# First k projections by contraction block, dummy matmuls ahead of them, 128-row transposes of the bias rows, and a newly planned order

## The chip, the core and the metric

The kernel runs on one core of one Trainium2 chip. The metric is the device time of one execution in microseconds, as the median of three runs. A core has five engines that run their own instruction streams side by side: TensorE (PE, matmuls; its weight loads are shown apart as PEld), VectorE (DVE), ScalarE (ACT), GpSimd (POOL) and SyncE (SP), which here does nothing but issue DMA transfers. The streams meet only at semaphores, and each is executed in order.

## The reference, cut to what matters

The input x has 2048 rows of 448 features. Two branches are computed from it and mixed row by row with a gate.

```python
g = sigmoid((x * gate_w).sum(-1, keepdims=True))

# branch A: 16 heads of 28, four segments of 512 rows
q, k, v = x @ wq, x @ wk, x @ wv
for s in range(4):
    p = softmax(q_s k_s^T * scale + causal mask)
    a_dot = p @ v_s
    a_mem = (phi(q_s) @ M) / (phi(q_s) @ z + 1e-6)
    o_s = sigmoid(beta) * a_mem + (1 - sigmoid(beta)) * a_dot
    M, z = M + phi(k_s)^T v_s, z + phi(k_s).sum(rows)
a = o @ wo

# branch B: a two-layer network over the row axis
h = layernorm(x)
u = gelu(h^T @ w1 + b1)        # 448 x 1792
b = (u @ w2 + b2)^T            # 2048 x 448

out = g * a + (1 - g) * b
```

## The kernel before

**A planner makes the order.** The program is written as about 1300 operations, each with an engine (some with a choice of two), the resources that it reads and writes, a cost in ns, a priority, and for a DMA its number of bytes. `Sched.plan` is a list scheduler: it walks through time, gives each engine the ready operation of lowest priority number, counts a TensorE operation double before `COLD` (3200 ns from its start), adds `SWITCH` where TensorE changes between full and packed matmuls, and lets a DMA land by one channel of 290 bytes per ns (L240 to L243). `SHIFTS` adds a number to the priority of single operations by name. The outcome is a fixed order of each engine's instructions, with the semaphore waits that the dependencies need. Nothing is decided on the chip: an engine whose next instruction waits stands still, with all that is behind it.

**The work.** Names as they are used below, with n counting tiles or groups:

- `ldx`, `ldwk`, `ldwq`, `ldwv`, `ldgw`, `ldb1`, `ldb2`, `ldbeta`, `ldwo`: loads of x (tiles of 128 rows), the weights, the gate's weights, biases and the rest. A weight of 448 rows comes in contraction chunks of 128 rows, the last one overlapping (`C0`): `ldwk0` brings chunks 0 and 1, `ldwk1` chunk 2, `ldwkb` chunk 3. `load_w` (L485) issues them on SP, with `ldwkb` alone on ACT's queue.
- `dtx1_0` to `dtx3_1` (`transpose_x`, L495): x transposed by DMA, 512 rows to a chunk (a chunk's three contraction blocks in `_0`, the fourth in `_1`). The first 512 rows are transposed by TensorE instead: `trx0_0` (row tiles 0 and 1) and `trx0_1` (tiles 2 and 3), each into two PSUM banks that `xTcp0_..` copies to SBUF (`transposes_0`, L628; DVE for contraction blocks 0 and 1, ACT for 2 and 3).
- `warm`, `warm2` (L595): seven and two dummy matmuls of 512 columns over a constant, into a bank that is not read.
- `padk`, `padx`, `padq` (L609): DVE spreads the weights' heads of 28 columns over 32, in chunks (`padk0` chunks 0 and 1, `padk1` chunk 2, `padk2` chunk 3).
- `prk`, `prq`, `prx` (`proj_d`, L655): projections of k, of q, and of the last heads of both, four heads to a group, by four matmuls over the contraction chunks. For the first 512 rows k is done in two halves of 256 (`prk0_n` and `prk0_nh`). One operation holds a group's four matmuls, so none of them starts before all chunks of the weights and both copies of the half are there. `cpk`, `cpq` evict them.
- `prt` (`do_v`, L743): v and the gate's sum, `wvx` carrying the gate's weights as column 448. They come from `gstage`, four rows of 128, by a TensorE transpose `gtr` (`do_gw`, L766) and the copies `gw`, `gwb`. `btr` (`do_small`, L805) does the same for the 30 rows of biases in `bstage`.
- `gk`, `gq`: heads of 28 columns leave the last four columns of each 32 free; these hold the heads that group 3 lacks, which are gathered through DRAM (four stores, then loads `_h0` to `_h2`), in two batches from SP.
- `ek`, `mk`, `phk`, `tk` and `eq`, `mq`, `phq`: phi of k and q on ACT and DVE, k's transposed by DMA (`tk`). `mst`, `msta`, `mstc`: the memory.
- `sc`, `exp`, `mask`, `pv`, `mem`, and the DVE chain `ta` to `ot`: attention by pairs of units (a unit is four heads of a segment). A pair's scores are filled in five steps `sc_0` to `sc_4`, each over the same four banks 0 to 3, which `exp` on ACT must have read before the next step; `mask` on POOL clears what is above the diagonal.
- `bns`, `bna`, `vpe`, `rstd`, `nmr`, `ln`: the layer norm, in place on x, on DVE (`rstd` on POOL).
- `u` and `y` (`mm1`, `mm2`): branch B, u by 14 blocks of 16 matmuls (one for each tile of x after `ln`), y by 16 of 14, with `gsq`, `gvh`, `garg`, `gth`, `gelu` as its GELU. Their weights pass through three ring slots, 1 MB (`ldw1_0` to `_6`) or 0.9 MB (`ldw2_0` to `_7`) a load. `wo`, `ag`, `fin`, `out` finish a row tile.

**The order around the change.** On TensorE: `warm`, `trx0_0`, `warm2`, `trx0_1`, then the k projections of the first 512 rows, half 0 (three groups) and half 1 (two), `prx0_3`, `prq0_0`, `prq0_1`, `gtr`, the last k half and the first v tiles. On SP: x tile 0, `ldwk0`, `ldwk1`, x tiles 2 and 3, wq, wv, the gate's weights, `dtx1`, x tiles 4 to 15, the biases, `ldbeta`, one part of wo, `ldw1_0`, then `tk0_0`, `tk0_1`, `dtx2`, `ldw1_1`, `dtx3_0` and the gathers. Until then, banks are dealt out in turn, 0 to 3 (`next_bank`, L589).

## Time and profile before

| what | value |
|---|---|
| median of the runs | 180.11 us (180.07 to 180.22) |
| the profiled execution, first to last instruction | 180.4 us |
| DVE busy | 151.0 us, 84% |
| ACT busy | 131.3 us, 73% |
| SP's queue: share of the 16 DMA engines' time | 53.1% |

The profile is of one execution of its own. Times in it count from its first instruction. In a list by time a row has the start, the length, the engine, the line of the kernel, the operation, what is written from what, and how many instructions are merged; in brackets is the idle time of the engine before it and what ended that. A matmul's length has some time of the pipeline in it, so rows of neighbours overlap. An SPq or ACTq row is the issue of a transfer, not the transfer.

The loads that feed the ring, as the page has them (KB each, median us from issue to landing):

```profile
t<-in_B_w_dram SPq DMA_DIRECT2D x7, 1024.0 KB, 6.2
```

### The profile page before, as it was taken

To read this page: it belongs to the slowest core of one execution; us is meant where nothing else is said; L and a number is where in the kernel's file an instruction comes from. 1 tells how busy PE (TensorE), PEld (TensorE's weight loads), DVE (VectorE), ACT (ScalarE), POOL (GpSimd) and SP (SyncE) were. 2 spreads that over 40 slices of the span, in tenths; PEclk is the share of its full clock that TensorE was granted. 3 is DMA by queue.
4 is the path that set the end of the run, shared out by engine and by line. 5 is a ranking of instruction groups with operands and counts; after the bars stand their busy time and mean duration, and the time that the engine had idled before them with its cause. 6 is when DMAs were issued, how large, how long until landed. Compare 5 with 4: busy or idle time off the path is not lost.

```text
span 180.4 us, 3443 instructions
## 1 busy us (share of the span) xinstructions
PE 174.0 (96%) x1300; PEld 83.3 (46%) x1313; DVE 151.0 (84%) x335; ACT 131.3 (73%) x161; POOL 71.1 (39%) x93
## 2 busy tenths in 40 slices
PE   8799998999999999999999999999999999999993
PEld 3454443444544544344544444444445444545562
DVE  2579989999898899999999797999798998983131
ACT  2267798899958999998999998987496977104100
POOL 7023111835503252436562727655632458520000
PEclk9999999999999999999999999999999999999999
DMA  5999997595581757121715241128731008394001
GB/s 160 261 292 300 129 271 162 136 253 134 156 231 33 221 155 153 25 51 40 207 57 147 71 136 29 48 66 228 202 89 37 14 4 254 95 320 125 22 29 51
DMA packets 49552, 24.32 MB, mean 135 GB/s; under 512 B 14384, under 2 KB 49296, under 8 KB 49536
## 3 DMA queue, kind: packets, MB, share of 16 engines
q1 hardware_dynamic: 49312, 23.93, 53.1%
q8 instruction: 10, 0.16, 0.4%
q10 hardware_dynamic: 224, 0.17, 0.3%
q14 instruction: 6, 0.05, 0.1%
HBM read 18.59 MB, written 2.36 MB: 116 GB/s over the span
## 4 chain that ended last, share of the span: by engine, by line
PE 67%; DVE 14%; ACT 13%; DMA 2%; issue 1%; SPq 1%
PE t L1032 23%; PE t L1004 20%; ACT t L905 8%; PE t L659 5%; PE t L984 5%; PE t L896 5%; PE t L933 5%; DVE t L839 3%; DMA t<-in_A_x_dram 2%; ACT t L1008 2%; DVE t L855 1%; PE t L749 1%; DVE t L684 1%; ACT t L1019 1%; DVE t L716 1%
## 5 line engine op out<-in xcount | busy, mean ns | idle before, releaser
L905 ACT ACTIVATE t<-t 128x2048 bf16<-128x2048 f32 x40 | 75.3, 1884 | 8.8 <-PE t L896 8.7
L908 POOL TENSOR_SCALAR_AFFINE_SELECT t<-t 128x512 bf16<-128x512 bf16 x64 | 46.9, 734 | 61.2 <-ACT t L905 50.6
L1004 PE MATMUL t<-t 128*128 128x448 bf16 x224 | 46.3, 353 | 0.4 <-DVE t L727 0.3
L1032 PE MATMUL t<-t 128*128 128x448 bf16 (+1 forms) x238 | 46.3, 342 | 0.3 <-DVE t L959 0.2
L1032 PEld LDWEIGHTS t<-t 128*128 128x128 bf16 x238 | 22.3, 98 | 19.7 <-issue 2.5
L1004 PEld LDWEIGHTS t<-t 128*128 128x128 bf16 x224 | 20.5, 98 | 20.8 <-issue 3.1
L659 PE MATMUL t<-t 128*128 128x512 bf16 (+1 forms) x118 | 27.6, 373 | 0.3
L1037 DVE SCALAR_TENSOR_TENSOR t<-t 128x448 bf16<-128x448 f32 (+1 forms) x17 | 10.9, 646 | 12.6 <-PE t L1032 12.6
L964 POOL TENSOR_TENSOR t<-t 128x448 bf16<-128x448 f32 x12 | 15.5, 1295 | 10.5 <-DVE t L962 10.5
L659 PEld LDWEIGHTS t<-t 128*128 128x128 bf16 x124 | 12.3, 104 | 11.7 <-issue 0.6
L896 PE MATMUL t<-t 28*128 28x512 bf16 (+3 forms) x256 | 15.8, 301 | 0.3 <-ACT t L763 0.2
L990 ACT ACTIVATE t<-t 128x448 bf16<-128x448 f32 x11 | 7.8, 726 | 10.6 <-PE t L984 10.5
L749 PE MATMUL t<-t 128*128 128x449 bf16 x64 | 14.4, 354 | 0.3 <-DVE t L684 0.3
L984 PE MATMUL t<-t 128*128 128x448 bf16 x64 | 13.3, 353 | 0.0
L949 DVE STREAM_TRANSPOSE t<-t 128x512 f32<-128x512 f32 x16 | 11.3, 704 | 0.9 <-PE t L933 0.8
L970 DVE STREAM_TRANSPOSE t<-t 128x512 bf16<-128x512 bf16 x16 | 11.1, 694 | 0.7 <-POOL t L964 0.7
L933 PE MATMUL t<-t 128*32 128x512 bf16 (+3 forms) x256 | 11.6, 302 | 0.0
L896 PEld LDWEIGHTS t<-t 28*128 28x128 bf16 x256 | 4.4, 92 | 14.0 <-ACT t L905 9.1
L1019 ACT ACTIVATE t<-t 128x448 f32<-128x448 f32 x14 | 8.1, 590 | 2.0 <-DVE t L1016 1.9
L947 DVE STREAM_TRANSPOSE t<-t 128x512 f32<-128x512 f32 x12 | 8.3, 694 | 1.4 <-remote 1.0
L1008 ACT ACTIVATE t<-t 128x448 f32<-128x448 f32 x14 | 8.9, 642 | 0.8 <-PE t L1004 0.8
L848 POOL TENSOR_TENSOR t<-t 128x4 f32<-128x4 f32 x4 | 4.5, 1138 | 12.4 <-DVE t L846 12.4
(81 smaller groups left out, 211.7 us busy)
## 6 DMA issues: line engine op xcount, KB each, us to landing
t<-in_B_w_dram SPq DMA_DIRECT2D x7, 1024.0 KB, 6.2
t<-in_B_w_dram SPq DMA_DIRECT2D x8, 896.0 KB, 5.3
out_dram<-t SPq DMA_DIRECT2D x15, 112.0 KB, 2.7
t<-in_A_x_dram SPq DMA_DIRECT2D x3, 448.0 KB, 5.0
t<-in_A_wo_dram SPq DMA_DIRECT2D x4, 98.0 KB
t<-in_A_wq_dram SPq DMA_DIRECT2D x1, 336.0 KB, 4.9
t<-in_A_wv_dram SPq DMA_DIRECT2D x1, 336.0 KB, 4.9
spare_heads<-t SPq DMA_DIRECT2D x8, 32.0 KB
```

Source lines behind the costliest of these rows:

```text
L659: last = e.matmul(bank(b)[:, 0:n], wqk[:, c, 4 * G : 4 * G + 4, :].rearrange("p h j -> p (h j)"), xT[0:CK, c, tc * 512 + t0 : tc * 512 + t ...
L749: last = e.matmul(bank(b)[:, 0 : D + 1], xT[0:CK, c, t * 128 : t * 128 + 128], wvx[0:CK, c, 0 : D + 1], start=(c == 0), stop=(c == NCT - 1 ...
L896: last = e.matmul(bank(hl)[:, c0 : c0 + w], kT[r, hg, s * 512 + j * 128 : s * 512 + j * 128 + 128], qT[r, hg, s * 512 + 128 * j : s * 512 ...
L905: op("ACT", lambda e: e.activation(pslot(g), ps[:, 0:4, :], ACT.Exp, scale=SCALE), reads=R_bank[0:4], writes=[g.res], take=g, name=f"exp{p ...
L908: op("POOL", lambda e, c0=c0: e.affine_select(pslot(g)[:, :, c0 : c0 + 128], pslot(g)[:, :, c0 : c0 + 128], pattern=[[0, 4], [1, 128]], co ...
L933: last = e.matmul(bank(cb)[32 * hl : 32 * hl + 32, 128 * j : 512], vaug[:, 4 * s + j, 32 * h : 32 * h + 32], pslot(P_fill[u // 2][f])[:, h ...
L949: dv(lambda e: e.transpose(t2[:, 0, :], bank(cb)[:, 0:512]), [bres(cb)], [R_tt[tb][0]], "ta", 630, use=(cb,))
L964: op("POOL", lambda e: e.tensor_tensor(o3, n3[0], n3[1], op=ALU.add), reads=R_tt[tb], writes=[R_ob[tb]], name=f"o{u}", cost=1280, port=Tru ...
L984: last = e.matmul(bank(b)[:, 0:D], oT[:, hg, T * 128 : T * 128 + 128], wo_sb[:, hg, :], start=(hg == 0), stop=(hg == NHG - 1), skip_group_ ...
L1004: op("PE", lambda e, st=st: e.matmul(bank(b)[:, 0:D], w1c[:, st, f2 * 128 : f2 * 128 + 128], xh[:, st, :], start=(st == 0), stop=(st == NT ...
L1008: op("ACT", lambda e: e.activation(gg[:, q, :], bank(b)[:, 0:D], ACT.Square, bias=b1s[:, ft : ft + 1], scale=math.sqrt(GC)), **buse(b), re ...
L1032: op("PE", lambda e, ft=ft: e.matmul(bank(b)[:, 0 : c1 - c0], w2c[:, ft, t2_ * 128 : t2_ * 128 + 128], uT[:, ft, c0:c1], start=(ft == 0), ...
```

## The change

Seven things are edited:

1. `warm2` goes. `fill` issues `NFILL` = 6 dummies of 256 columns, each an operation of its own and of the highest priority number, released at 3000 ns of the plan.
2. `do_k_first` takes the place of the first three `do_k`: for each of the three groups an operation for contraction chunks 0 and 1, one for chunk 3 and one for chunk 2, each waiting for its own chunk of weights and its own copy of x alone.
3. `xTcp0_..` may run on either ACT or DVE. The banks of the first operations are dealt out by the list `EARLY`.
4. `bstage` and `gstage` have 128 rows, cleared by DVE, and `btr` and `gtr` are plain matmuls against columns of the identity, over 128 rows and into float32.
5. `ldwk1` is issued on ACT.
6. The planner's model of DMA and of the start: `COLD` 5500, the channel 350 bytes per ns with a stretch around 2400 ns in which 1200 ns are added, a least time for each DMA (`dmin`: 5900 for the w1 loads, 5300 for w2), other bytes and costs for the transposing DMAs.
7. A new `SHIFTS` of some 150 entries. With 6 it makes another order of nearly all operations.

The new order begins, on TensorE: `warm`, `trx0_0`, six fills, the three pieces of k group 0, `trx0_1`, the pieces of groups 1 and 2 interleaved, the three k groups of half 1, `prq0_0`, `prq0_1`, `prk1_0`, `prx1_3`, `prq0_2`, `prk1_1`, `prk1_2`, `prq1_1`, `prq1_2`, `prx0_3`, four matmuls of `u0`, `prq1_0`, `btr`, `gtr`, four of `u1`, `prk2_0`, `prk2_1`, seven v tiles, four of `u0`, `prt7`, `sc0_0`, twelve of `u2` and `u0`, `sc0_1`, four of `u2`, seven of `u1`, `sc0_2`, and after ten more the last matmul of `u0`.

On SP: `ldx0`, `ldwk0`, `ldx2`, `ldwq0`, `dtx1_1`, `ldwqb`, `ldwvb`, `ldwv0`, `dtx1_0`, `ldx8`, `ldgw`, `ldx4`, `ldb1`, `ldb2`, `ldw1_0`, `dtx2_0`, `dtx2_1`, `ldbeta`, `ldwo1`, `ldwo3`, `ldgwb`, `ldw1_1`, `ldx12`, `dtx3_1`, `tk0_0`, `gk0_3`, `gq0_1`, `gq0_2`, `gq0_3`, `gk0_2`, `ldwo2`, `tk0_1`, `ldwo0`, `gq0_0`, `gk0_1`, `ldw1_2`, `gk0_0`, `tk0_2`, `gq0_h0` to `_h2`. On ACT the Exp of q `eq1_3`, which reads what `gq0_h0` to `_h2` bring, stands between `exp0_1` and `exp0_2`. On POOL the four `rstd` come ahead of the first mask.

```diff
...
 SWITCH = 97.0
+NFILL = 6
 HOLD = 2500.0
-COLD = 3200.0
+COLD = 5500.0
+DMA = (350.0, 1000.0, 950.0, 2400.0, 1200.0)
 LAT = {"PE": 163.0, "ACT": 120.0, "DVE": 83.0, "POOL": 50.0, "SP": 0.0}
...
             if o.nbytes:
-                chan = max(chan, t + 1090.0) + o.nbytes / 290.0
-                o.end = max(t + 1900.0, chan + 850.0)
+                before = chan
+                chan = max(chan, t + DMA[1]) + o.nbytes / DMA[0]
+                if before <= DMA[3] < chan:
+                    chan += DMA[4]
+                o.end = max(t + o.dmin, chan + DMA[2])
             else:
...
 SHIFTS = (
-    ("cpk3_3", 15.1), ("dtx3_0", -0.43), ("dtx3_1", 146.0), ("gk2_1", 0.63), ("gq0_0", 7.37), ("gq3_h2", 215.59),
-    ("gth7", 7.61), ("gvh10", 14.61), ("gvh11", -0.19), ("ldbeta", 0.27), ("ldw1_3", 235.85), ("ldwk0", -64.28),
...
+    ("b2c", -26.38), ("b2g1", -67.36), ("bna15", 153.62), ("bna7", 36.31), ("bna9", -16), ("bns0", -77.77),
+    ("bns11", 305.8), ("bns12", 26.86), ("bns13", 149.7), ("bns14", 137.06), ("bns15", 19.55), ("bns7", 190.26),
+    ("bns8", 297.6), ("bns9", 126.67), ("cpq3_3", 2.95), ("cpv10", 207.44), ("cpv8", 230.42), ("dtx1_0", -72.24),
+    ("dtx1_1", -344.5), ("dtx3_0", 1654.44), ("dtx3_1", 84.56), ("ek1_0", 17.16), ("ek1_1", 117.41),
...
     ident = sb([128, 128])
-    bstage = sb([NFT + NT, 128])
-    gstage = sb([NCT, 128])
+    bstage = sb([128, 128])
+    gstage = sb([128, 128])
     betab = sb([128, H])
...
         for k, (c0, c1) in enumerate(((0, 2), (2, 3)) if len(r) == 3 else ((0, 3),)):
-            op("SP", lambda e, c0=c0, c1=c1: e.dma_start(
+            op("ACT" if name == "wk" and k else "SP", lambda e, c0=c0, c1=c1: e.dma_start(
                 dst()[:, c0:c1, 0:D], src[128 * c0 : 128 * c1].rearrange("(c p) d -> p c d", p=128)),
...
                take=None if k else take)
-        op("SP" if take is not P_wk else "ACT", lambda e: e.dma_start(dst()[64:128, 3, 0:D], src[384:448]),
+        op("ACT" if name == "wk" else "SP", lambda e: e.dma_start(dst()[64:128, 3, 0:D], src[384:448]),
            writes=[r[-1]], name="ld" + name + "b",
...
                 xT[:, c : c + n, tc * 512 : tc * 512 + 512], x2[tc * 512 : tc * 512 + 512, C0[c] : C0[c] + 128 * n]),
-               writes=[R_xT[tc][k]], name=f"dtx{tc}_{k}", dma=True, cost=1200 * n, nbytes=227000 * n, prio=-1 if tc == 2 else -3 if tc == 1 else 0)
+               writes=[R_xT[tc][k]], name=f"dtx{tc}_{k}", dma=True, cost=700 * n + 500, nbytes=150000 * n + 40000, prio=-1 if tc == 2 else -3 if tc == 1 else 0)
...
     load_w(lambda: wvx, WV, R_wv, "wv")
+    for st, rs, name in ((gstage, R_gst, "g"), (bstage, R_bst, "b")):
+        op("DVE", lambda e, st=st: e.memset(st[:].bitcast(U32), 0), writes=rs, name="sz" + name, cost=120, prio=-5.0)
     op("SP", lambda e: e.dma_start(gstage[0:3, :], GW[0:384].rearrange("(c p) -> c p", p=128)),
...
                reads=R_wv, writes=[R_slot[r]], name=f"ldw1_{k}", dma=True, cost=500,
-               nbytes=1320000, prio=(-2.5, -0.5)[k] if k < 2 else 0)
+               nbytes=1048576, dmin=5900.0, prio=(-2.5, -0.5)[k] if k < 2 else 0)
         else:
...
                                            w2v[:, :, j * 256 : j * 256 + 256]),
-               writes=[R_slot[r]], name=f"ldw2_{j}", dma=True, cost=500, nbytes=1155000)
+               writes=[R_slot[r]], name=f"ldw2_{j}", dma=True, cost=500, nbytes=917504, dmin=5300.0)
...
     early = [True]
+    EARLY = (0, 1, 2, 0, 1, 3, 2, 0)
...
             rr[0] += 1
-            return (rr[0] - 1) % 4
+            return EARLY[rr[0] - 1] if rr[0] <= len(EARLY) else (1, 3, 2, 0)[(rr[0] - 1 - len(EARLY)) % 4]
         return Bank()
...
     warm_up(7, "warm", -1)
-    warm_up(2, "warm2", P_PROJ + 0.01, 3500.0)
+
+    def fill(n):
+        for i in range(n):
+            op("PE", lambda e: e.matmul(bank(3)[:, 0:256], ones[:, 0:128], ones[:, 0:256], start=True, stop=True,
+                                        skip_group_check=True),
+               writes=[R_bank[3]], name=f"fill{i}", mode="f", cost=pe_cost(256), prio=1e4, rel=3000.0)
+
+    fill(NFILL)
...
-            if k == 0:
-                op("DVE", lambda e, io=io: e.tensor_copy(*io()), **buse(bs[k]), reads=[bres(bs[k])], writes=[R_xT0[half][k]],
-                   name=f"xTcp0_{half}{k}", cost=dve_cost(512, 2), prio=P_PROJ - 150)
-            else:
-                op("ACT", lambda e, io=io: e.activation(*io(), ACT.Copy), **buse(bs[k]), reads=[bres(bs[k])], writes=[R_xT0[half][k]],
-                   name=f"xTcp0_{half}{k}", cost=act_cost(512), prio=P_PROJ - 150)
+            op("ACT", lambda e, io=io: e.activation(*io(), ACT.Copy), **buse(bs[k]), reads=[bres(bs[k])],
+               writes=[R_xT0[half][k]], name=f"xTcp0_{half}{k}", cost=act_cost(512), prio=P_PROJ - 150,
+               alt=("DVE", lambda e, io=io: e.tensor_copy(*io()), dve_cost(512, 2)))
...
            cost=act_cost(n), prio=P_BASE, alt=("DVE", lambda e: e.tensor_copy(ks, bank(b)[:, 0:n]), dve_cost(n)))
+
+    def do_k_first():
+        banks = [next_bank() for _ in range(3)]
+        for i, (cs, k) in enumerate((((0, 1), 0), ((3,), 2), ((2,), 1))):
+            for hg in range(3):
+                def fn(e, cs=cs, hg=hg):
+                    last = None
+                    for c in cs:
+                        last = e.matmul(bank(banks[hg])[:, 0:256],
+                                        wqk[:, c, 4 * hg : 4 * hg + 4, :].rearrange("p h j -> p (h j)"),
+                                        xT[:, c, 0:256], start=(c == 0), stop=(c == 2), skip_group_check=True)
+                    return last
+
+                op("PE", fn, reads=[R_xT0[0][i > 0], R_wkp[k], R_wkp[3 + k]], writes=[bres(banks[hg])],
+                   name=f"prk0_{hg}c{i}", mode="f", cost=pe_cost(*[256] * len(cs)), prio=PRJ[0] - 1)
+        for hg in range(3):
+            ks, b = kT[:, hg, 0:256], banks[hg]
+            op("ACT", lambda e, ks=ks, b=b: e.activation(ks, bank(b)[:, 0:256], ACT.Copy), reads=[bres(b)],
+               writes=[R_kT[hg][0]], name=f"cpk0_{hg}", cost=act_cost(256), prio=P_BASE,
+               alt=("DVE", lambda e, ks=ks, b=b: e.tensor_copy(ks, bank(b)[:, 0:256]), dve_cost(256)))
...
                                                  kphi[:, p, :]),
-           reads=[R_kphi[p]], writes=[R_phk[tc][hg]], name=f"tk{tc}_{hg}", dma=True, cost=600, prio=-2, nbytes=500000)
+           reads=[R_kphi[p]], writes=[R_phk[tc][hg]], name=f"tk{tc}_{hg}", dma=True, cost=1200, prio=-2, nbytes=400000)
...
         b = next_bank()
-        gps = ps[:, b, 0:2].bitcast(BF16)
-        op("PE", lambda e: e.matmul(gps, gstage[:, :], ident[0:NCT, 0:NCT], is_transpose=True, start=True, stop=True,
-                                    skip_group_check=True),
+        gps = ps[:, b, 0:NCT]
+        op("PE", lambda e: e.matmul(gps, gstage[:, :], ident[:, 0:NCT], start=True, stop=True, skip_group_check=True),
            reads=R_gst + [R_ident], writes=[bres(b)], name="gtr", mode="f", cost=60, prio=P_PROJ - 1)
...
         pr = P_PROJ - 20
-        bps = ps[:, b, 0:15].bitcast(BF16)
+        bps = ps[:, b, 0 : NFT + NT]
...
-        op("PE", lambda e: e.matmul(bps, bstage[:, :], ident[0 : NFT + NT, 0 : NFT + NT], is_transpose=True,
-                                    start=True, stop=True, skip_group_check=True),
+        op("PE", lambda e: e.matmul(bps, bstage[:, :], ident[:, 0 : NFT + NT], start=True, stop=True,
+                                    skip_group_check=True),
            reads=R_bst + [R_ident], writes=[bres(b)], **btake(b), name="btr", mode="f", cost=100, prio=pr, rel=15000.0)
...
     pool_clears()
-    for t0 in (0, 256):
-        for hg in range(3):
-            do_k(0, hg, t0, 256)
+    do_k_first()
+    for hg in range(3):
+        do_k(0, hg, 256, 256)
     pad_q()
```

5 lines of the change are left out of this document (3 added, 2 removed), and 31 rows, old and new, of the table SHIFTS.

## The prediction

> **What bounds the kernel now.** I read the page's totals and its chain of waits first, then TensorE's busy time by stage, then the first 14 us instruction by instruction, because that is where TensorE is not working.
>
> ```profile
> span 180.4 us, 3443 instructions
> PE 174.0 (96%) x1300; PEld 83.3 (46%) x1313; DVE 151.0 (84%) x335; ACT 131.3 (73%) x161; POOL 71.1 (39%) x93
> PEclk9999999999999999999999999999999999999999
> PE 67%; DVE 14%; ACT 13%; DMA 2%; issue 1%; SPq 1%
> ```
>
> TensorE is busy 96% of the span and holds 67% of the chain of waits.
>
> ```profile
> 12.00:30.00 18.00, 17.28 (x93) 1.00 1.18 242
> 30.00:100.00 70.00, 69.51 (x566) 1.00 0.51 130
> 100.00:160.00 60.00, 59.52 (x492) 1.00 0.40 107
> ```
>
> The first number of a stage is its length, the second TensorE's busy time. From 12 to 160 us TensorE idles 0.72 + 0.49 + 0.48 = 1.7 us. It is the bound, and an order of the same work can give back 1.7 us there at most. The rest of the waste is at the start:
>
> ```profile
> 0.82 3.15 PE L599 MATMUL t<-const-bfloat16-1.0 128*128 128x512 bf16 x7 [0.82 <-PEq L1157]
> 3.76 1.06 PE L636 MATMUL t<-t 128*128 128x128 bf16 x8
> 4.62 1.06 PE L599 MATMUL t<-const-bfloat16-1.0 128*128 128x512 bf16 x2
> 6.65 1.04 PE L636 MATMUL t<-t 128*128 128x128 bf16 x8 [0.97 <-DMA t<-in_A_x_dram]
> 7.48 6.26 PE L659 MATMUL t<-t 128*128 128x256 bf16 x31
> ```
> ```profile
> 7.48:10.03 2.55, 2.55 (x12) 1.00 1.20 234
> 9.50:10.00 0.50, 0.50 (x4) 1.00 1.28 283
> 10.50:11.00 0.50, 0.50 (x7) 1.00 0.75 149
> ```
> ```profile
> 45.29 8.81 PE t L1004 x46
> 74.31 1.77 ACT t L905
> 166.83 10.64 PE t L1032 x70
> ```
>
> Twelve 256-column matmuls fill 2.55 us, 0.213 each. Late in the kernel 46 of 448 columns take 8.81 us: 0.192 each, so 0.109 for 256 columns, 0.055 for 128, 0.219 for 512. TensorE runs at half rate until a point between the two half-microsecond slices (4 matmuls against 7), about 10.2 us. The granted clock reads 1.00 throughout and does not show this; the counts do. The last matmul ends at 166.83 + 10.64 = 177.5; the 2.9 us of output behind it stay.
>
> **When the rate doubles.** The burst from 0.82 to about 5.5 us does not bring it, though it is 4.6 us long; the work from 6.65 does, 3.5 us after its start. Both fit if the rate is decided over stretches of one length L, each of which must be busy throughout, with an edge at 10.2: L is at most 3.5, and no whole stretch may fit between 0.82 and 5.5, which leaves L from 3.1 to 3.5 and the edge before at 6.7 to 7.1. The stretch ending there holds the 0.97 us in which TensorE waits for x tiles 2 and 3. If it were busy, the rate would double at about 6.8. The runs differ by 0.15 us, so the edges seem to sit still against the kernel's start.
>
> [...]
>
> **The change, part by part.**
>
> *Fills and the first k projections.* The built order becomes: seven dummies, transposes of tiles 0 and 1, six 256-column dummies, the three contraction pieces of k group 0, and only then the transposes of tiles 2 and 3.
>
> ```profile
> 4.55 0.72 DVE L610 COPY t<-t 128x392 bf16<-128x392 bf16 x4 [2.39 <-DMA t<-in_A_wk_dram]
> 5.92 0.35 DVE L610 COPY t<-t 128x392 bf16<-128x392 bf16 x2 [0.65 <-DMA t<-in_A_wk_dram]
> 6.18 0.42 DVE L649 COPY t<-t 128x512 bf16<-128x512 bf16 x1
> 8.92 0.82 DVE L610 COPY t<-t 128x224 bf16<-128x224 bf16 x4
> 4.86 0.60 ACT L652 ACTIVATE t<-t 128x512 bf16<-128x512 bf16 x1 [1.79 <-PE t L636]
> ```
>
> Fills: 4.62 + 6 x 0.213 = 5.90. The first piece needs xTcp0_00, now on ACT (4.86 + 0.60 = 5.46), and DVE's copies of weight chunks 0 and 1: 0.72 of pads plus the other 0.42 of xTcp0 from 4.55 gives 5.7. Both are ready. Four pieces at 0.213 end at 6.75; the last needs chunk 2, whose pads end at 6.27 today. Tiles 2 and 3 land by 6.65 and are wanted at 6.75. No gap, so the rate doubles at 6.8. By then eight transposes and four matmuls are done, 8 x 0.055 + 4 x 0.109 = 0.88 us at full rate; before, by 10.2, sixteen and 12.7: 2.26 us. Gain (10.2 - 2.26) - (6.8 - 0.88) = 2.0 us. Bounds: 1.85 to 2.1 with the edge at 7.1 or 6.7; 0.4 if the doubling stays at 10.2 (then only three more matmuls are done by it). The two memsets on DVE fall into its 2.39 us of waiting; without that cover they would cost some 0.2. Chunk 2's load moves to ACT, idle until 4.86.
>
> *Small transposes over 128 rows.*
>
> ```profile
> 13.67 0.09 PEld L769 LDWEIGHTS t<-t 4*128 4x128 bf16 x1 [0.42 <-issue]
> ```
>
> The gate weights' load of 4 rows holds TensorE's weight loads for 0.42 us with nothing to wait for; the bias rows' load has the same form, and I price it alike. The new ones, of 128 rows, look like their neighbours. Matmuls in flight hide most of the 0.42: between 0 and 0.2 each, I take 0.1 (near the lower end, since TensorE itself shows no idle time there): gain 0.2.
>
> *Weight pads for q.* wqb is issued behind a transposed load (about 4.0 instead of 3.2), and the pads end at 9.74 today. TensorE wants prq0_0 at 6.8 + 0.44 + 20 x 0.109 = 9.4. Wait 0 to 0.7, I take 0.3.
>
> *SP's order.* SP issues in order, so each step moved delays what is behind it.
>
> ```profile
> 0.78 0.40 SPq L482 DMA_DIRECT2D t<-in_A_x_dram  x1
> 5.81 2.84 SPq L497 DMA_TRANSPOSE t<-in_A_x_dram  x2
> 12.51 0.39 SPq L535 DMA_DIRECT2D t<-in_B_w_dram  x1
> 16.16 2.52 SPq L719 DMA_TRANSPOSE t<-t  x2
> 18.73 3.74 SPq L497 DMA_TRANSPOSE t<-in_A_x_dram  x2
> 22.52 0.58 SPq L535 DMA_DIRECT2D t<-in_B_w_dram  x1
> 23.15 4.48 SPq L497 DMA_TRANSPOSE t<-in_A_x_dram  x1
> 27.68 4.14 SPq L693 DMA_DIRECT2D spare_heads<-t  x7
> 34.07 2.13 SPq L693 DMA_DIRECT2D spare_heads<-t  x1
> ```
> ```profile
> DMA to landing us min/median/max: 2.5/4.3/5.7
> ```
>
> (The last line is the x loads'.) Five of the 19 issues ahead of ldw1_0 leave, at 0.5 each (ten from 0.78 to 5.81): it goes out at 10.0. Right behind it now come both transposed loads of chunk 2 (3.74), ldbeta and two wo loads (0.59 each), then ldgwb at about 15.9, which lands 2.5 to 4.3 later, 18.4 to 20.2. TensorE reaches gtr, which needs it and which all matmuls stand behind, at 6.8 + 0.44 + 20 x 0.109 + 44 x 0.219 + 4 x 0.192 + 0.3 = 20.1. Further on: ldw1_1, ldx12, dtx3_1, tk0_0, five gathers and a wo load, tk0_1, three more, ldw1_2, gk0_0 (2.13 like the row at 34.07), tk0_2 (half of 2.52) and three head loads (0.59 each): issued by 32.2, landed at 34.7. ACT needs them for eq1_3, which stands ahead of exp0_2; it gets there at 34.3: sc0_1 ends at 20.1 + 52 x 0.192 + 8 x 0.219 + two score fills at 0.33 = 32.5, exp0_1 takes 1.77. No margin; I take 0.4 of wait for both places, between 0 and 4.0 (third rival).
>
> *DVE's order.*
>
> ```profile
> 9.74:39.34 29.60, 27.21 (x91) 1.00 1.03 223
> ```
> ```profile
> 37.58 1.77 DVE L855 TENSOR_SCALAR t<-t 128x448 bf16<-128x448 bf16 x4
> ```
> ```profile
> L762 DVE CAST t<-t 128x448 bf16<-128x448 f32 x3 | 1.8, 604 | 0.0
> L716 DVE SCALAR_TENSOR_TENSOR t<-t 128x512 bf16<-128x512 bf16 x2 | 1.3, 674 | 0.0
> L714 DVE TENSOR_SCALAR t<-t 128x512 bf16<-128x512 bf16 x2 | 0.5, 266 | 0.0
> ```
>
> From the last q pad (8.92 + 0.82 = 9.74) to the last normalisation ln15 (37.58 + 1.77 = 39.34) DVE has 90 instructions and idles 2.4 us. In the new order there are 97: seven evictions of 0.60 to 0.69 leave, four of 0.67, four of 0.27 and six of about 0.17 come, the same sum within 0.2. With today's idle time ln15 would end at 39.3 plus the wait for the pads, without it at 36.9. TensorE wants it at the sixteenth u0 matmul, 32.5 + 21 x 0.192 + 0.33 = 36.9 (before, that matmul stood behind other work). Between 0 and 2.4 of wait; I take 0.5, near the lower end, because part of today's idle time is waiting for a TensorE that now comes earlier.
>
> *The rest of the order.* TensorE's matmuls are the same but for the dummies, and the changes between full and packed matmuls are 97 in both orders. POOL now has all four rstd ahead of its first mask, which must then wait for DVE's vpe12; that mask isn't read before pv0, which stands four score fills later, so I take nothing, and up to the 0.5 above if DVE is late. The 0.72 us of idle time from 12 to 30 belongs to an order that is gone: gain 0.5, between 0 and 0.7. From 40 us on I take nothing, within 1.0 either way: ACT and DVE leave TensorE there as little margin as before, and one ring slot is short of it (ldw2_3 can go out when y1 ends, about 6 us before y7; loads of that kind need 5.3 by the page).
>
> ```profile
> t<-in_B_w_dram SPq DMA_DIRECT2D x8, 896.0 KB, 5.3
> ```
>
> **Sum.** 180.4 - 2.0 - 0.2 - 0.5 + 0.3 + 0.4 + 0.5 = 178.9 us of span. The median of the runs lies 0.3 under the profiled span, so 178.6.
>
> **The rivals.**
>
> 1. *The rate still doubles at 10.2*, because chunk 2 or the x tiles land late enough to leave a gap in the stretch, or because dummies and transposes count otherwise than I think. For it: chunk 2 now shares the queues with other loads. Against: the margins above. The gain is then 0.4 of the 2.0, but TensorE reaches the places of waiting 1.6 later and loses none of the 1.2 there: 180.4 - 0.4 - 0.2 - 0.5 = 179.3, median 179.0; with the plan out of step by as much, I say 179.4.
>
> 2. *DVE takes the place of the cold clock.* The full 2.4 us of wait at ln15 in place of 0.5: 178.6 + 1.9 = 180.5, less what the waits at SP's places then no longer cost (0.4): 180.1. For it: DVE is busy 92% of that stage. Against: its idle time of today is not all its own.
>
> 3. *SP is held behind the 1 MB loads: slower.* The transposed load at 23.15 stands right behind a w1 load and takes 4.48 to issue; a single gather behind the next w1 load takes 2.13. Now dtx2_0 stands right behind ldw1_0, and dtx3_1 two behind ldw1_1. If dtx2_0 takes 4.48 and its partner 1.26, against 3.74 for the pair, ldgwb is 2.0 later and TensorE stands still at gtr; if dtx3_1 is held another 2.0, the heads for eq1_3 are late again, exp0_2 with them, and the score banks. 2.0 to 4.0 in all, 2.9 taken, in place of 0.4: 178.6 + 2.5 = 181.1. It decides from a lateness of some 1.9 us on. For it: the two rows. Against: the load at 16.16 behind ldw1_0 ran at its usual pace, though 3.6 us later.
>
> **How the numbers follow.** Forecast 178.6, chance 0.42, with its own range 177.3 to 179.6; first rival 0.13; second 0.17; third 0.28. The range reaches from 177.0 (every gain at its bound and no new wait: 180.4 - 2.1 - 0.4 - 0.7 - 0.3 = 176.9) to 181.6 (three quarters of the third rival's upper price), some 2 in 10 left out. About 0.2%, 0.4 us, is what can be told from no change: faster is under 179.75, slower over 180.47. Faster: 0.41 of the forecast, 0.10, 0.06 and 0.03 of the rivals, together 0.60. Slower: 0.23 of the third, 0.03 of the second, 0.02 of the others, 0.28. The same: 0.12.
>
> **What would show it.** Right: the count of k matmuls per half microsecond rises near 6.8 and TensorE has no idle time from 0.82 to then; gtr and the last u0 wait less than 0.5 each. Wrong: half rate up to 10 (first); idle time before a u0 matmul ended by a DVE normalisation near 37 (second); a dtx issue of over 4 us behind a w1 load, idle time before the 4-column gate matmul, or ACT idle before an Exp over qT until the head loads land (third). A gap of some microseconds after 40 us, at a ring load, would be none of these and would make the prediction wrong.

## The result, and the profile after

The changed kernel takes 186.38 us (median of 4 runs, 185.40 to 186.71) against 180.17 us before (180.07 to 180.27): a ratio of 1.033, 95% interval 1.030 to 1.036. The forecast of 178.6 us, and its range up to 181.6, are missed on the slow side. Below, a median is of all executions, and a ratio leaves out those that took over 1.5% longer than the fastest of the same kernel.

The changed kernel's page, its totals and its chain of waits:

```profile
span 184.8 us, 3440 instructions
PE 172.7 (93%) x1304; PEld 81.7 (44%) x1317; DVE 149.0 (81%) x333; ACT 133.7 (72%) x165; POOL 71.7 (39%) x93
PE 65%; DVE 14%; SPq 8%; DMA 8%; issue 2%; ACT 1%; DVEq 0%
```

TensorE (96% busy before) is at 93%, and SP's queue and DMA, 3% of the chain before, now hold 16% of it. TensorE by stage (length, busy time):

```profile
12.00:30.00 18.00, 16.35 (x80) 1.00 1.10 222
30.00:100.00 70.00, 65.79 (x533) 1.00 0.59 135
100.00:160.00 60.00, 58.76 (x504) 1.00 0.32 89
```

It idles 1.65, 4.21 and 1.24 us where it idled 0.72, 0.49 and 0.48. Of the 4.21, 4.05 lie ahead of 45 us. What it waits for between 12 and 60 us (instruction waiting, what ended the wait, us in all, times, longest):

```profile
PE t L1053 <- DVE t L904: 3.0, 3, 1.4
PE t L862 <- ACT t L732: 1.6, 1, 1.6
PE t L945 <- ACT t L954: 0.9, 1, 0.9
```

L1053 is a `u` matmul waiting for a normalised row tile (`ln`), L862 is `btr`, whose bank `cpq0_3` must free, L945 a score step behind an Exp. The same view of VectorE and of ScalarE shows that these two wait first, for transfers:

```profile
DVE t L888 <- DMA t<-in_A_x_dram: 3.2, 1, 3.2
DVE t L786 <- ACT t L784: 1.8, 1, 1.8
DVE t L871 <- ACT t L869: 1.2, 1, 1.2
```
```profile
ACT t L784 <- DMA t<-spare_heads: 3.0, 1, 3.0
ACT t L762 <- DMA t<-t: 2.3, 1, 2.3
ACT t L869 <- DMA t<-in_A_beta_dram: 1.6, 1, 1.6
```

The transfers are late at SP, which issues almost without a pause from 4 to 39 us (at most 0.19 us between two rows of its list). From the list by time of its queue (start, length, line):

```profile
10.90 0.38 SPq L560 DMA_DIRECT2D t<-in_B_w_dram  x1
11.33 6.55 SPq L520 DMA_TRANSPOSE t<-in_A_x_dram  x2
17.92 0.58 SPq L542 DMA_DIRECT2D t<-in_A_beta_dram  x1
20.00 0.39 SPq L560 DMA_DIRECT2D t<-in_B_w_dram  x1
20.43 2.20 SPq L505 DMA_DIRECT2D t<-in_A_x_dram  x1
33.17 0.45 SPq L560 DMA_DIRECT2D t<-in_B_w_dram  x1
33.67 2.08 SPq L743 DMA_DIRECT2D spare_heads<-t  x1
37.19 1.12 SPq L748 DMA_DIRECT2D t<-spare_heads  x3
```

Behind each of these 1 MB loads (L560) the next issue is long: 6.55 for the pair `dtx2_0`, `dtx2_1`, 2.20 for the x load `ldx12`, 2.08 for one gather. The changed planner costs the first of the pair at 2.6 us (700 x 3 + 500) and an x load at 0.5. `ldbeta` goes out at 17.92, the heads for `eq1_3` at 37.19. The x load that starts at 20.43 lands 8.26 us later; the x loads of the kernel before took 2.5 to 5.7. The chain of waits runs through them:

```profile
20.43 8.26 DMA t<-in_A_x_dram
28.71 0.63 DVE t L888
...
36.31 0.69 DVE t L789
...
38.35 1.39 SPq L520
...
40.40 2.03 DMA t<-spare_heads
42.43 1.77 ACT t L954
```

From the x load through VectorE's statistics and phi of q to SP, the last head load, an Exp and the score step at 44.25.

### The profile page after: what moved, and what is told of

Same layout as the page of the kernel before. It is cut to its first block, busy times and chain, and to the rows that moved or that the text cites. A ratio compares the mean times of both kernels' runs of the same rounds, so it can differ in the third digit from the quotient of the medians.

```text
span 184.8 us, 3440 instructions
## 1 busy us (share of the span) xinstructions
PE 172.7 (93%) x1304; PEld 81.7 (44%) x1317; DVE 149.0 (81%) x333; ACT 133.7 (72%) x165; POOL 71.7 (39%) x93
## 4 chain that ended last, share of the span: by engine, by line
PE 65%; DVE 14%; SPq 8%; DMA 8%; issue 2%; ACT 1%; DVEq 0%
PE t L1081 21%; PE t L1053 19%; PE t L1033 7%; PE t L945 6%; SPq L520 5%; PE t L982 5%; DMA t<-in_A_x_dram 4%; PE t L799 3%; DMA t<-in_A_wq_dram 2%; PE t L689 2%; PE t L833 2%; DVE t L888 1%; DVE t L904 1%; DMA t<-spare_heads 1%; DVE t L777 1%
## 5 line engine op out<-in xcount | busy, mean ns | idle before, releaser
L957 POOL TENSOR_SCALAR_AFFINE_SELECT t<-t 128x512 bf16<-128x512 bf16 x64 | 48.3, 756 | 52.9 <-ACT t L954 49.1
L1053 PE MATMUL t<-t 128*128 128x448 bf16 x224 | 48.2, 353 | 3.3 <-DVE t L904 3.0
L1053 PEld LDWEIGHTS t<-t 128*128 128x128 bf16 x224 | 20.1, 98 | 25.0 <-DVE t L904 5.0
L1081 PEld LDWEIGHTS t<-t 128*128 128x128 bf16 x238 | 22.3, 98 | 19.4 <-issue 2.5
L689 PE MATMUL t<-t 128*128 128x512 bf16 (+1 forms) x107 | 23.9, 367 | 0.3
L1013 POOL TENSOR_TENSOR t<-t 128x448 bf16<-128x448 f32 x12 | 14.9, 1245 | 13.9 <-DVE t L1011 10.2
L1039 ACT ACTIVATE t<-t 128x448 bf16<-128x448 f32 x12 | 8.7, 728 | 13.1 <-PE t L1033 13.0
L945 PE MATMUL t<-t 28*128 28x512 bf16 (+3 forms) x256 | 15.8, 301 | 1.1 <-ACT t L954 0.9
L689 PEld LDWEIGHTS t<-t 128*128 128x128 bf16 x112 | 10.4, 98 | 11.8 <-issue 0.6
L1033 PE MATMUL t<-t 128*128 128x448 bf16 x64 | 13.9, 353 | 0.5 <-DVE t L1019 0.2
L799 PE MATMUL t<-t 128*128 128x449 bf16 x64 | 13.5, 353 | 0.0
L888 DVE BATCH_NORM_STATS2 t<-t 128x6 f32<-128x448 bf16 x16 | 9.7, 609 | 3.3 <-DMA t<-in_A_x_dram 3.2
L897 POOL TENSOR_TENSOR t<-t 128x4 f32<-128x4 f32 x4 | 4.1, 1025 | 20.4 <-DVE t L895 20.4
L998 DVE STREAM_TRANSPOSE t<-t 128x512 f32<-128x512 f32 x16 | 11.1, 701 | 0.5 <-PE t L982 0.5
L1070 DVE SCALAR_TENSOR_TENSOR t<-t 128x448 bf16<-128x448 f32 x14 | 10.3, 739 | 0.5 <-ACT t L1068 0.2
L945 PEld LDWEIGHTS t<-t 28*128 28x128 bf16 x256 | 4.5, 92 | 14.0 <-ACT t L954 9.5
L784 ACT ACTIVATE t<-t 128x512 bf16<-128x512 bf16 x12 | 7.5, 631 | 3.1 <-DMA t<-spare_heads 3.0
```

Of the source, the lines that this page charges most:

```text
L689: last = e.matmul(bank(b)[:, 0:n], wqk[:, c, 4 * G : 4 * G + 4, :].rearrange("p h j -> p (h j)"), xT[0:CK, c, tc * 512 + t0 : tc * 512 + t ...
L799: last = e.matmul(bank(b)[:, 0 : D + 1], xT[0:CK, c, t * 128 : t * 128 + 128], wvx[0:CK, c, 0 : D + 1], start=(c == 0), stop=(c == NCT - 1 ...
L888: op("DVE", lambda e: e.bn_stats(st6[:, t, :], xh[:, t, :]), reads=[R_x[t]], writes=[R_st6[t]], name=f"bns{t}", cost=512, prio=P_PROJ - 10 ...
L945: last = e.matmul(bank(hl)[:, c0 : c0 + w], kT[r, hg, s * 512 + j * 128 : s * 512 + j * 128 + 128], qT[r, hg, s * 512 + 128 * j : s * 512 ...
L957: op("POOL", lambda e, c0=c0: e.affine_select(pslot(g)[:, :, c0 : c0 + 128], pslot(g)[:, :, c0 : c0 + 128], pattern=[[0, 4], [1, 128]], co ...
L998: dv(lambda e: e.transpose(t2[:, 0, :], bank(cb)[:, 0:512]), [bres(cb)], [R_tt[tb][0]], "ta", 630, use=(cb,))
```

## The experiments

In the table, "busy" is VectorE's and TensorE's busy time in the 48 us from 12 to 60 us. Ratios are against the kernel before as it ran beside each.

| run | median us | ratio, 95% interval | span of its profile | VectorE busy | TensorE busy |
|---|---|---|---|---|---|
| before (page, repeat) | 180.17 | | 180.4, 178.6 | 45.4, 44.8 | 47.2, 47.3 |
| changed | 186.38 | 1.033 (1.030 to 1.036) | 184.8 | 39.2 | 42.3 |
| x12_ahead | 186.70 | 1.030 (1.021 to 1.039) | 184.9 | 39.4 | 42.5 |
| beta_ahead | 187.46 | 1.033 (1.026 to 1.040) | 185.3 | 38.4 | 41.8 |
| both_ahead | 187.81 | 1.033 (1.022 to 1.043) | 186.9 | 36.5 | 41.6 |
| heads_later | 187.39 | 1.036 (1.027 to 1.045) | 186.4 | 38.4 | 42.5 |
| heads_later_loads | 187.48 | 1.033 (1.024 to 1.041) | 185.4 | 38.6 | 41.6 |
| ops_old_order_new | 186.49 | 1.032 (1.026 to 1.038) | 186.7 | 37.3 | 42.3 |
| front_only | 190.02 | 1.047 (1.039 to 1.054) | 188.4 | 45.4 | 47.7 |
| ops_new_order_old | 182.91 | 1.012 (1.006 to 1.018) | 180.8 | 45.4 | 46.3 |
| ops_new_order_old_b | 182.43 | 1.007 (1.003 to 1.011) | 180.1 | 45.0 | 46.7 |
| hold_before | 180.98 | 1.000 (0.997 to 1.004) | 178.3 | 44.9 | 47.2 |
| replay_swap | 182.08 | 1.006 (1.001 to 1.010) | 180.2 | 45.1 | 46.8 |
| more_three | 183.69 | 1.018 (1.010 to 1.026) | 181.7 | 45.5 | 45.2 |
| more_six | 185.18 | 1.021 (1.011 to 1.032) | 183.9 | 45.5 | 44.1 |
| more_six_b | 184.54 | 1.018 (1.012 to 1.024) | 183.1 | 46.1 | 44.1 |
| more_in_wait | 187.17 | 1.040 (1.029 to 1.050) | 184.6 | 42.4 | 42.5 |
| tuned_new | 182.74 | 1.010 (1.007 to 1.013) | 181.0 | 45.1 | 46.6 |
| tuned_old | 181.11 | 1.000 (0.996 to 1.003) | 179.7 | 44.4 | 46.7 |

### One late transfer after the other is put right

`move` takes one operation out of its engine's planned order and puts it ahead of another; `reorder` does so with several.

```diff
+    sch.move("ldx12", "ldw1_0")
```

x12_ahead: 

> The changed kernel with one DMA moved: ldx12 issued ahead of ldw1_0, as in the kernel before, all other orders kept. If the late x tiles 12 to 15 are the chain, DVE's 3.2 us of waiting for them goes, the u0 to u2 matmuls idle 1 to 2 us in place of 4.9, and the span falls by 2 to 3.5 from 184.8; ldw1_0 lands 1.3 later and may cost up to 1 of it. If SP's queue is not the cause, it stays within 0.5 of 184.8.

```diff
+    sch.move("ldbeta", "ldw1_0")
+    sch.move("ldgwb", "ldw1_0")
```

beta_ahead: 

> The changed kernel with ldbeta and ldgwb issued ahead of ldw1_0, all else kept. TensorE's 1.76 us of idle time at the bias transpose (held by ACT, which waits for beta) falls under 0.4. But the x tiles still land near 29, so if these are the chain TensorE only waits longer at u0 and the span falls by under 0.6; if the bias transpose is the chain it falls by 1.5.

both_ahead has all three moves: 

> ldx12, ldbeta and ldgwb all ahead of ldw1_0. If the held queue is the cause, the two savings add: span 180.0 to 181.5, that is 3.5 to 5 under the changed kernel. If the new order is worse for other reasons, it stays above 183.

None is shown to be faster than the changed kernel: all three intervals cover its 1.033, and the 3.5 us or more expected of both_ahead are excluded. In x12_ahead VectorE's wait for x is gone, and a wait of the same length stands behind the gate's row (`omgh` behind `tb`), because `ldbeta` now goes out later; the numbers of lines differ by 11:

```profile
DVE t L882 <- ACT t L880: 3.2, 1, 3.2
```

With both groups ahead, phi of k (L775) and phi of q (L797) are what VectorE waits for: ScalarE's `ek` waits for a transposed DMA, its `eq` for the head loads. And TensorE waits for something new, the 1 MB load `ldw1_0` itself, which has been put behind the moved loads (11.92 instead of 10.90):

```profile
DVE t L775 <- ACT t L773: 3.1, 1, 3.1
DVE t L797 <- ACT t L795: 2.6, 1, 2.6
PE t L1064 <- DMA t<-in_B_w_dram: 1.6, 1, 1.6
```

That takes the place of the 1.6 us at `btr`, which are gone. So these moves on SP's full queue had a price of their own.

Then I took the head loads' readers out of the way.

```diff
+    sch.reorder("ACT", ("eq1_3", "ek1_0", "ek0_3"), "gsq1")
+    sch.reorder("DVE", ("mq1_3", "mk1_0", "phq1_3", "phk1_0", "mk0_3"), "garg0")
+    sch.resort()
```

heads_later: 

> The changed kernel with ScalarE's eq1_3, ek1_0 and ek0_3 put behind exp0_3, and VectorE's mq1_3, mk1_0, phq1_3, phk1_0 and mk0_3 put behind ln15; SyncE's order as in the changed kernel. Theory A (the head loads come late on SyncE, and what costs is that instructions which wait for them stand ahead of exp0_2, exp0_3 and ln15): TensorE's idle of 1.10 us at 42.6 and 0.91 us at 44.2 goes, the idle before that (1.59 at 21.6, 1.42 at 31.5) stays; time 1.4 to 2.4 us below the changed kernel's 186.4, so 184.0 to 185.0. Rival B (what costs is the late x and beta loads alone): within 0.5 us of the changed kernel.

```diff
+    sch.reorder("SP", ("ldx12", "ldbeta", "ldgwb"), "ldw1_0")
```

heads_later_loads has both: 

> The same, and ldx12, ldbeta and ldgwb put ahead of ldw1_0 on SyncE. Theory A: both groups of waits are needed to see either; with both gone TensorE idles under 1.5 us between 12 and 45 us, time 181.5 to 183.2. Rival B: like the runs with the loads moved alone, 186.7 to 187.8. Rival C (TensorE would wait for something else in this stretch, as both orders are bound by the pace of ScalarE's exps): 184.5 to 186.5, with TensorE idle over 2.5 us between 30 and 45 us.

Theory A fell; the number of heads_later_loads is that of its rival B. The waits at 42 to 45 us go, but one of 2.3 us comes between 46 and 50 us, where a `u` block's bank waits for a VectorE that now has the delayed phi work in front of it. TensorE's and VectorE's longest waits in heads_later_loads (L1078 is `u`):

```profile
PE t L1078 <- DVE t L1088: 2.3, 1, 2.3
PE t L1078 <- DMA t<-in_B_w_dram: 1.9, 1, 1.9
DVE t L789 <- ACT t L787: 3.0, 2, 2.7
```

Each of these waits can be moved; TensorE's idle time from 12 to 60 us stays at 5.5 to 6.4 us in these five kernels, VectorE's busy time at 36.5 to 39.4 of 48, and their time stays where it was.

### Operations or order

front_only is edits 1 to 5 with the planner's numbers and the `SHIFTS` of before (the diff is against the changed kernel).

```diff
-COLD = 5500.0
+COLD = 3200.0
...
+    ("cpk3_3", 15.1), ("dtx3_0", -0.43), ("dtx3_1", 146.0), ("gk2_1", 0.63), ("gq0_0", 7.37), ("gq3_h2", 215.59),
```

> The changed program's operations (fills, k by contraction block, 128-row transposes, choice of engine for the copies) with the planner's DMA model and SHIFTS of before, so that SP's order is that of before. If SP's order is what costs (dtx2_0 held 5.25 us behind ldw1_0), dtx2_0 takes about 2.4 here, TensorE idles under 1 us from 12 to 45 us and the time is 178 to 179.8, below the kernel before. If the fills and the split projections themselves cost, or the order of everything else does, it is 182 or more.

It gave 190.02 us and tells nothing of that question: its planner made a third order, which idles little to 100 us and stands still near the end. TensorE, list by time:

```profile
168.99 5.86 PE L1013 MATMUL t<-t 128*128 128x448 bf16 x16 [5.47 <-DVE t L999]
```

The last units' results reach `wo12` 5.47 us late, and its 16 matmuls then take 5.86 us where the 46 of the forecast's row took 8.81, so 3.06 for 16.

For a clean answer the planner was made to replay given orders: each engine takes the next name of its list, and the planner only deals out banks.

```diff
+ORDER = {
+    "PE": """
...
-                           if not o.take or sum(v[0] <= t for v in banks[o.take[0].pool].values()) >= len(o.take)]
+                           if slot[o.idx] == turn[e] and (not o.take or sum(v[0] <= t for v in banks[o.take[0].pool].values()) >= len(o.take))]
```

ops_old_order_new, the old operations in the new order: 

> The operations of the kernel before in the order of the changed kernel on every engine; warm2 stands where the dummies stand, and each k projection where its last block stands. Theory: as the changed kernel or slower by what its start gains, ratio 1.033 to 1.05, TensorE idle of 5 us or more between 12 and 45 us. Rival (the operations are the cause): ratio 0.995 to 1.01.

ops_new_order_old, the new operations in the old order: 

> All changed operations (k projections by contraction block, six dummy matmuls, small rows over 128 rows, the second part of wk on ScalarE's queue), but every engine keeps the order of the kernel before; only the new names stand in the place of the old ones. Theory (the operations gain at the start, the new order loses between 12 and 45 us): TensorE idles under 2.5 us in all, the first 12 us hold some 2 us less excess, time 1.0 to 2.5 us below before, ratio 0.986 to 0.995. Rival (the operations themselves cost, by the transposes over 128 rows or the dummies): ratio over 1.005.

In this last kernel the two halves of `cpk0_0` had changed places. ops_new_order_old_b puts them right:

```diff
-            e, i = next(x for x in where[o.name] if x[0] in o.alts)
+            e, i = next(x for x in sorted(where[o.name], reverse=o.name == "cpk0_0") if x[0] in o.alts)
```

> As ops_new_order_old, mended: there the two halves of cpk0_0 had changed places (ScalarE copied the first half, in the place of the second), here VectorE copies the first and ScalarE the second, as in the kernel before. Theory (the operations neither gain nor lose much, as before's rate mostly doubles at about 4.3 us too): ratio 0.996 to 1.004. Rival (the operations themselves cost): 1.008 or more. Rival (they gain 2 us, as forecast): 0.986 to 0.992.

replay_swap is the kernel before with the swap alone: 

> The kernel before with one edit: the two halves of cpk0_0 change places as in ops_new_order_old, more_six and more_three. It is the kernel against which more_six and more_three are to be read. Theory (the late copy of the first half makes TensorE wait at 9.2 and 14.1 us, as in those runs): 0.8 to 2.2 us more than before, and more_three and more_six then cost 1.5 to 2.5 and 2.8 to 4.2 us by their VectorE work. Rival (the swap is free): within 0.4 us of before.

The order alone costs 3.2% (2.6 to 3.8), as much as the whole change. The operations alone cost 0.7% (0.3 to 1.1), neither the gain of the forecast nor nothing; the swap alone 0.6%. The 0.7% stand in a part of the executions only: of the twelve, the six with a granted clock of 0.998 to 1.000 took 180.90 to 181.81 us, beside 181.17 for the kernel before, and the six with 0.991 or less took 183.05 or more. Of the 23 of the kernel before, one had such a clock. Why the new operations meet it more often is open; the only trace kept is of an execution at 1.00. The old operations in the new order show the changed kernel's three kinds of wait on TensorE (L1088 is `u`, L897 `btr`, L980 a score step):

```profile
PE t L1088 <- DVE t L939: 3.4, 3, 1.8
PE t L897 <- ACT t L766: 1.2, 1, 1.2
PE t L980 <- ACT t L989: 0.9, 1, 0.9
```

### Is a late transfer enough?

hold_before gives the kernel before the place of `dtx2` in the new order.

```diff
+    sch.reorder("SP", ("dtx2_0", "dtx2_1"), "tk0_0")
```

> The kernel before with one edit: dtx2_0 and dtx2_1 put right behind ldw1_0, ahead of tk0_0 and tk0_1. Theory (the first transfer that SyncE issues behind a 1 MB load is held until most of that load is done): dtx2_0 takes 4.5 to 5.5 us at SyncE instead of the 2.5 us that it had behind tk0_1, dtx2_1 1.2 to 1.4, tk0_0 is issued 19.0 to 19.8 instead of 16.2; time 0 to 1.0 us more than before. Rival (the length is that of the transposed load itself, wherever it stands): dtx2_0 takes 2.3 to 2.7 us, time within 0.3 us of before.

SP's list by time:

```profile
12.51 0.38 SPq L560 DMA_DIRECT2D t<-in_B_w_dram  x1
12.94 8.44 SPq L522 DMA_TRANSPOSE t<-in_A_x_dram  x2
21.42 2.58 SPq L744 DMA_TRANSPOSE t<-t  x2
24.04 0.58 SPq L560 DMA_DIRECT2D t<-in_B_w_dram  x1
```

The hold is even longer than expected, 8.44 us for a pair that took 3.74 in the page of before, and `tk0_0` goes out 5.3 us later than there. The time does not change (0.997 to 1.004), and VectorE stays at 44.9. So this one hold does not make the old order slower. It is no full copy of the new order's trouble, though. In the page of before SP stood idle from 12.90 to 16.16, ahead of `tk0_0`, and the hold fills that time: `ldw1_1` and what follows go out only some 1.5 us later (24.04 against 22.52), and x and beta are as early as before. A late x load or late heads were not tried in the old order.

### What a lost microsecond of VectorE costs

The kernels of the table without added work are in two groups: VectorE busy for 44.4 us or more between 12 and 60, or for 39.4 or less. That does not say which engine lost its time first, since a kernel that is 5 us behind at 60 us has less of every engine's work in the stretch, and TensorE's column falls alike. To see whether VectorE's time is what counts, bn_stats that read x again and write to a scratch were added, each 0.575 us from start to start.

```diff
+MORE = (4, 5, 6, 7, 4, 5)
...
+                op("DVE", lambda e, i=i: e.bn_stats(more[:, i, :], xh[:, t, :]), reads=[R_x[t]], writes=[R(f"more{i}")],
+                   name=f"more{i}", cost=512)
```

more_three: 

> The same with three more bn_stats, 1.7 us of VectorE work. Theory: half the price of six, 0.9 to 1.8 us more than before. Rival: 0 to 0.4 us more.

more_six: 

> The kernel before, each engine in its own order, with six more bn_stats on VectorE (they read x again and write to a scratch that nothing reads), put ahead of bna6 at about 20 us: 6 times 0.575 = 3.5 us more VectorE work. Theory (VectorE has hardly any slack between 12 and 60 us, so what it loses there is lost on the time, as the changed order loses 6 us of it by waits): 2.3 to 3.5 us more than before, ratio 1.013 to 1.020, and TensorE idles 2 to 3.5 us more between 20 and 60 us. Rival (VectorE stands off the path that sets the end, as the forecast took it): 0 to 0.8 us more.

Both carry the swap of `cpk0_0` too. more_six_b is without it: 

> As more_six, mended in the same way: the kernel before, every engine in its own order, and nothing but the six more bn_stats on VectorE at about 20 us. Theory (VectorE has hardly any slack between 12 and 60 us): 2.3 to 4.2 us more than before, ratio 1.013 to 1.023. Rival (VectorE stands off the path): 0 to 0.8 us more.

more_six_b costs 1.8% (1.2 to 2.4), some 3.2 us for 3.45 us of VectorE work. Against replay_swap, more_three and more_six cost 1.2% and 1.6% (differences of two ratios from different sets of runs, with no interval of their own), 2.2 and 2.9 us for 1.7 and 3.45. Where it is lost can be read in more_six_b. From its chain of waits and, last, from TensorE's list by time:

```profile
20.35 3.15 DVE t L935 x6
...
24.30 0.08 DVE t L902
```
```profile
24.44 0.94 PE L834 MATMUL t<-t 128*128 128x449 bf16 x4 [2.66 <-DVE t L902]
```

L935 is the added work, L902 (`b2c`) the last copy out of `btr`'s bank, and L834 a v tile that needs this bank. The six instructions stand just ahead of the copies that free a bank, and TensorE stands still for 2.66 us at once.

The reverse is more_in_wait, the changed kernel with the same six instructions in its wait for x:

```diff
+MORE = (8, 9, 10, 11, 8, 9)
```

> The changed kernel, each engine in its own order, with six more bn_stats on VectorE ahead of bns15, where it waits 3.2 us for the x load. Theory (what counts is VectorE's lost time, not its work): the work goes into the wait, 0 to 0.8 us more than the changed kernel, ratio to before 1.030 to 1.037. Rival (VectorE's work itself counts wherever it stands): 2.5 to 3.5 us more, ratio 1.045 to 1.052.

VectorE works 3.2 us more, and the profiled span is 184.6 against 184.8. The ratio's interval is wide: it covers the changed kernel's and reaches into the rival's 1.045 to 1.052. Its two executions with a granted clock of 1.00 took 186.36 and 186.35, as long as the changed kernel (186.38); the two with 0.991 took 187.97 and 188.73. So the added work most likely went into the wait. In the wait it cost next to nothing (186.36 against 186.38 us), and at 20 us of the old order, where VectorE has none to spare, nearly its length (3.2 us for 3.45). This fits the reading that what counts is VectorE's time, lost by work or by waiting, but does not show it: the work was added at one place of the old order only, and there a bank stood behind it. VectorE's busy time over the same 48 us:

```profile
12.00:60.00 48.00, 45.37 (x131) 1.00 0.81 182
```
```profile
12.00:60.00 48.00, 39.20 (x121) 1.00 0.90 185
```
```profile
12.00:60.00 48.00, 46.06 (x130) 1.00 0.85 188
```

Before, changed, more_six_b. The last has 3.45 us of added work in it, so 42.6 of the kernel's own.

### The start

before_again is the kernel before, profiled once more: 

> The kernel before without any edit, profiled once more. Theory (the instant at which TensorE's instructions become twice as fast differs between executions of one kernel, and the profile that the forecast was made from was a late one): TensorE's start to start of the two dummies and the transposes halves between 4.2 and 6.7 us instead of 10.2, the span is 178.0 to 178.8. Rival (it belongs to this kernel's start): 10.2 again, span 180.2 to 180.6.

```profile
3.76 0.87 PE L636 MATMUL t<-t 128*128 128x128 bf16 x8
4.47 0.60 PE L599 MATMUL t<-const-bfloat16-1.0 128*128 128x512 bf16 x2
6.47 0.62 PE L636 MATMUL t<-t 128*128 128x128 bf16 x8 [1.41 <-DMA t<-in_A_x_dram]
```

The two dummies start 0.21 us apart instead of 0.42, the second lot of transposes takes 0.62 instead of 1.04: the unchanged kernel doubled its rate during the first transposes (0.71 us from their start to the dummies', instead of 0.86), at about 4.2 us, and its span is 178.6. The changed kernel did so at about 4.3 us (0.77 from start to start; its six dummies take 0.83 in all).

### An order with slack

tuned_new has the operations of front_only, tuned_old those of before, each with about 620 shifts found by a search over the planner's own model, with longer issues behind 1 MB loads (here a first row of tuned_old's).

```diff
 SHIFTS = (
-    ("cpk3_3", 15.1), ("dtx3_0", -0.43), ("dtx3_1", 146.0), ("gk2_1", 0.63), ("gq0_0", 7.37), ("gq3_h2", 215.59),
+    ("ag0", -17.17), ("ag1", -23.98), ("ag10", 101.93), ("ag11", 504.64), ("ag12", 89.75), ("ag13", -138.46),
```

tuned_new: 

> The changed operations with the planner's model of before and a set of shifts that was searched so that the order keeps its time when SyncE's transfers behind a 1 MB load are held 1.7 to 2.1 us (transposed 3.9 to 4.5) and the other engines are up to 2 per cent slower. Theory (an order with slack against held loads keeps the gain of the start): ratio 0.975 to 0.995, TensorE idle under 2.5 us. Rival (the operations cost, or the order of before cannot be bettered): 1.0 to 1.01.

tuned_old: 

> The operations of the kernel before with shifts searched in the same way: the control for tuned_new. Theory: before idles 3.5 us, and an order can win back 1 to 2 of them, ratio 0.99 to 1.0, and tuned_new stands 1 to 2 us below it. Rival (the operations give nothing): tuned_new and tuned_old within 0.5 us.

Both expectations failed. The new operations lose 1.0% even in an order that keeps VectorE busy for 45.1 us, and the search wins nothing on the old ones. No kernel of the study beats the one before.

## Why the prediction was wrong

**What fell first: the two waits of the order, mis-sized by a factor of five.** The sum had 0.4 us for SP's order ("No margin; I take 0.4") and 0.5 for DVE's ("between 0 and 2.4 of wait; I take 0.5, near the lower end"). TensorE idles 5.70 us between 12 and 60 in place of 0.77: 4.9 where 0.9 were priced, and where -0.5 was booked for the old order's idle time. At the places of SP's term stand 2.5 of it (1.59 at `btr`, 0.91 at a score step), at those of DVE's term 3.0 (1.42, 0.49 and 1.10 ahead of `u` matmuls). The step that failed for SP is the reckoning of its issue times: `ldgwb` at 15.9 went out at 19.52, and the heads, issued by 32.2 and landed at 34.7, were issued by 38.31 and let `eq1_3` start at 41.28. The step that failed for DVE is what its term is made of. It weighed VectorE's work, 27.21 of 29.60 us, and let it never wait for a transfer. `ldx12`, moved from ahead of `ldw1_0` to behind `ldw1_1`, is in the forecast's list of SP's issues without a wait of its own; VectorE waits 3.2 us for it, and the `u` matmul at 31.48 waits behind that. That the new order carries the whole loss is shown by ops_old_order_new.

**The third rival had the mechanism at less than half the price.** Its signs are all but one there: `dtx2_0` and its partner held for 6.55 us (5.74 expected), ScalarE 3.0 us idle ahead of `eq1_3`, a score step waiting behind an Exp. TensorE did not stand at `gtr` but one place earlier, at `btr`, whose bank waits for `cpq0_3`, which stands on ScalarE behind `tb` and its late `ldbeta`. The second rival's sign is there as well, 3.0 us before `u` matmuls behind `ln`. The forecast priced the two as alternatives, up to 181.1 and 180.1; in the run they add up, 2.5 and 3.0 us at different matmuls. The held transposed load alone is not enough, as hold_before shows in the old order; here x, beta and the heads are late with it. And the forecast's hope that a wait in one place would spare another (rivals 1 and 2 subtract it) is what the moves of single loads show from the other side: a wait taken away comes back elsewhere, in part because the moved load makes `ldw1_0` late.

**The start: the right event, the wrong base.** The doubling came early, 4.3 us instead of the 6.8 forecast, in spite of an idle 0.82 us at 5.4 (TensorE waits for VectorE's weight pads, which the sum held to be in time). That is luck as well: kernels with the same first instructions doubled between 4.1 (both_ahead) and some 7 us (heads_later_loads). And the profile from which the gain of 2.0 was reckoned was an execution with a late doubling. "The runs differ by 0.15 us, so the edges seem to sit still against the kernel's start" is the step that failed: the repeat of the same kernel doubles at 4.2 and has a span 1.8 us shorter. "The median of the runs lies 0.3 under the profiled span" is the same error: in every run that has both, the device time is 1.7 to 1.8 us above the span (186.53 and 184.8, 180.3 and 178.6). The page's execution of 180.4 would read 182.1, two us above the median that it was taken for. Like for like, spans, the change costs 184.8 - 178.6 = 6.2: 5.0 between 12 and 60 us, 0.6 from 60 to 165, and by difference some 0.6 at the start. So the gain of 2.0 did not come either. The stretches of one length, from which the forecast had its 6.8, were an estimate from a single trace; no run shows them. What the runs show is that the doubling comes at 10.2 us in one execution of the kernel before and at about 4.2 in another.

**The small terms.** The wait for q's pads (0.3) did not come: TensorE has no idle time before `prq0_0`. The small transposes' 0.2 can't be told apart in any run. "From 40 us on I take nothing" missed 2.5 us of idle time between 40 and 45, the last part of the chain above; they are in the 4.9 already, as the late waits of the two terms. Clearing the bias rows and POOL's order show nowhere among TensorE's waits.

**What stays open.** Why the new order keeps losing 5 to 6 us of TensorE's time, whichever wait is taken away, was not brought down to one place; that it does is shown. Whether VectorE's lost time is the cause, or follows from several late transfers at once, is not decided: no kernel has the new order with all of x, beta, the heads and `ldw1_0` in time.

## What to carry to other kernels

When a new order puts several transfers behind each other, follow each one to its reader, give each its wait, and add up those that stand at different instructions instead of taking the longest. Where a second engine has as little to spare in the bound engine's stretch as VectorE here (busy for 45.37 of 48 us), take it as likely that a microsecond which it is made to wait is lost, above all ahead of the copies that free a bank (2.66 us at once in more_six_b). Look at what the issuing queue had to spare: the old order took a hold of 8.44 us with some 1.5 us of delay for what followed, as SP had stood idle there, and the new one had no such time to give. And profile the base twice before reckoning a gain from its first microseconds, and compare like with like, span with span.
